# Attention with cluster masks and two expert layers: the first key tile's transposed probabilities split on Pool, and the reciprocals' broadcast in one operation

## The chip, the cores and the metric

The kernel runs on one core of one Trainium2 chip. The core has five engines that run side by side, each through its own list of instructions in order: TensorE (PE in the rows, with its weight loads as PEld), VectorE (DVE), ScalarE (ACT), GpSimd (Pool, POOL in the rows) and SyncE (SP, which only issues DMAs here). An engine that waits for another holds up everything behind the waiting instruction in its own list. The metric is the device time of one execution in microseconds, lower is better.

## What is computed

```python
# attention: q, k, v of (2, 8, 768, 64), centroids of (8, 16, 64)
q_assign = argmax(einsum('bhsd,hcd->bhsc', normed(q), normed(centroids)))   # k_assign likewise
mask = q_assign[:, :, :, None] == k_assign[:, :, None, :]
scores = where(mask, q @ k.T / sqrt(64), -1e9)
attn = exp(scores - max(scores)); attn = attn / (sum(attn) + 1e-9)
x = (attn @ v)                       # put together to 1536 tokens x 512
# expert layer 1, w_in 512 x 2048, w_out 2048 x 512
h = x @ w_in;  x = (h * cos(h)) @ w_out
# expert layer 2, same sizes
h = x @ w_in2; g = where(h >= 1, h, where(h <= -1, 0, (h + 1)**2 / 4)); out = g @ w_out2
```

## The kernel before

Matrix products are made in a 32-bit format that PE rounds its inputs to (FP32R). To keep precision each operand is split into a high part (the number rounded to that format) and a low part (the number less its high part), and the products of the parts are summed in PSUM. So almost every operand needs two operations ahead of its matmul: a rounding copy and a subtraction.

The attention stage goes over 8 pairs of heads (2 batches, 4 pairs each, numbered from 0). A pair is prepared (`prep_pair`): the queries and keys are transposed and split, their dot products with the centroids are made (`dots`), the largest is found and made into one-hot rows (`eq`, L382 on DVE, L383 on Pool; `dots`, L390 on DVE), these are transposed on PE (`po`, L410) and copied by ACT (`oht`, L430) into the score operands, and the values are split on Pool (`vv`, L403 and L404).

Then come 4 units of a pair: one head and one half of the 768 query rows (384) each, 32 units in all, numbered through. A unit has six slots, one for each tile of 128 keys (`kt` 0 to 5). What a unit needs: scores in PSUM (`s`, L453 and L456 on PE), the row maxima (`nm`, L462 on DVE), the exponentials with their row sums (`p`, `den`, L471 on ACT), and in each slot three transposes of the probabilities into one PSUM tile of 128 x 384 (`pt`, L499 on PE), its high part (`phi`, L502, a copy by ACT) and its low part (`plo`, L507, a subtraction on DVE that reads the PSUM tile again), and two matmuls of `vv` with these parts that sum into `o` (L517, L518). The PSUM pool of these tiles has three buffers, which `pt`, `po` and some others share. The loop over slots runs ahead: scores are made 8 slots before the slot whose transposes need them, and the weighted sums (`p_v`) stand 4 slots or less behind their transposes, as PV_AT says:

```python
        PV_AT = (4, 4, 5, 6, 7, 8)
```

At the end of a unit `inverse` adds the small constant to the three row sums on Pool (`den`, L481), takes their reciprocals on DVE (L482), and spreads each over 64 columns on Pool (`rb`, L486, three operations). When both heads of a pair are through one half, `finish` transposes `rb` on PE (`r`, L541), adds the two parts of the result on Pool (`xt`, L543), multiplies by the transposed reciprocals on DVE (`xt`, L544), and splits the product on Pool (`xh`, L547; `xl`, L551).

The order in which an engine meets these is not that of the code alone: a scheduler puts each engine's list in order from the loop's order and its own idea of durations, so a changed instruction can move others. Preparing a pair begins 12 slots before the pair's first unit, so that its last steps (`eq`, `vv`, `po`) fall together with the finishing of the pair before: this stretch, six times in the run, is called a change of pairs here, and named by the pair that is being prepared.

Behind attention come the two expert layers (L603 on), dense matmuls with the hidden products split on Pool and DVE; the 64-bit weights are converted by DVE, ACT and Pool on the way (L134 to L161), two chunks of them already during attention.

Of the kernel before, what the change touches and what calls it, by code (L numbers as in the profile page):

```python
# [8 lines left out]
F32 = mybir.dt.float32  # L9
# [4 lines left out]
AF = mybir.ActivationFunctionType  # L14
ALU = mybir.AluOpType
# [3 lines left out]
P = 128  # L19
# [13 lines left out]
def attention_moe_moe(  # L33
# [18 lines left out]
    nc = tc.nc  # L52
    B, H, S, D = q.shape
# [3 lines left out]
    NJ = S // P  # L57
    HJ = NJ // 2
    HS = S // 2
# [9 lines left out]
    cpool = ctx.enter_context(tc.tile_pool(name="cpool", bufs=1))  # L69
# [2 lines left out]
    desc = cpool.tile([P, C], F32, name="desc")  # L72
    for c in range(C):
        nc.gpsimd.memset(desc[:, c:c + 1], float(C - c))
    ones = cpool.tile([P, D], F32, name="ones")
    nc.gpsimd.memset(ones, 1.0)
    ohscale = cpool.tile([P, 1], F32, name="ohscale")
    ohbias = cpool.tile([P, 1], F32, name="ohbias")
    for r in range(4):
# [25 lines left out]
    def later(n, f, *args):  # L105
        due.setdefault(now[0] + n, []).append((f, args))
# [85 lines left out]
    with ExitStack() as actx:  # L192
        ap = actx.enter_context(tc.tile_pool(name="apool", bufs=1))
# [271 lines left out]
        def row_exp(n):  # L465
            s, nm = ptile[n]
            u, jj = divmod(n, HJ)
            if jj == 0:
                dens[u] = ap.tile([P, HJ, 2], F32, tag="den", bufs=4, name=f"den{u}")
            p = ap.tile([P, 2, HS], F32, tag="p", bufs=P_BUFS, name=f"p{n}")  # L470
            nc.scalar.activation(p, s[:, :, :HS], AF.Exp, bias=nm,  # L471
                                 accum_out=dens[u][:, jj, 0:1])
            ptile[n] = p
            if jj == HJ - 1:
                later(2, inverse, u)

        def inverse(u):

            i, h, hf = units[u]
            den = dens.pop(u)  # L480
            nc.gpsimd.tensor_scalar(den[:, :, 0], den[:, :, 0], 1e-9, 1.0, ALU.add, ALU.mult)  # L481
            nc.vector.reciprocal(den[:, :, 1], den[:, :, 0])  # L482
            if h == 0:
                rb[(i, hf)] = ap.tile([P, HJ, 2, D], F32, tag="rb", bufs=2, name=f"rb{i}_{hf}")
            for jj in range(HJ):
                nc.gpsimd.tensor_scalar(rb[(i, hf)][:, jj, h], ones, den[:, jj, 1:2], 1.0,  # L486
                                        ALU.mult, ALU.mult)

        dens = {}
        rb = {}  # L490
# [4 lines left out]
        def p_transpose(u, kt):  # L495
            ps = ps_t.tile([P, HS], F32, tag="t", name=f"pt{u}_{kt}")
            for jj in range(HJ):
                p = ptile[u * HJ + jj].rearrange("p a n -> p (a n)")
                nc.tensor.transpose(ps[:, jj * P:(jj + 1) * P], p[:, kt * P:(kt + 1) * P], ident)  # L499
            hi = ap.tile([P, HS], F32R, tag="phi", bufs=6, name=f"phi{u}_{kt}")  # L500
            lo = ap.tile([P, HS], F32R, tag="plo", bufs=6, name=f"plo{u}_{kt}")
            nc.scalar.activation(hi, ps, AF.Copy)  # L502
            pts[(u, kt)] = (hi, lo, ps)

        def p_lo(u, kt):
            hi, lo, ps = pts[(u, kt)]
            nc.vector.tensor_tensor(lo, ps, hi.bitcast(F32), ALU.subtract)  # L507

        def p_v(u, kt):
            i, h, hf = units[u]  # L510
            vv = prepped[i][0]
            hi, lo, _ = pts.pop((u, kt))
            if kt == 0:
                opsum[u] = ps_o.tile([P, HS], F32, tag="o", name=f"o{u}")
            o = opsum[u]
            lhs = vv[:, kt, h * P:(h + 1) * P]
            nc.tensor.matmul(o, lhs, hi, start=(kt == 0), stop=False)  # L517
            nc.tensor.matmul(o, lhs, lo, start=False, stop=(kt == NJ - 1))  # L518
            if kt == NJ - 1:
                later(1, o_parts, u)  # L520

        def o_parts(u):
# [31 lines left out]


        LEAD, PREP, PREP1 = 8, 12, -3
        PV_AT = (4, 4, 5, 6, 7, 8)
        NSLOT = len(units) * NJ
        PAIR = 4 * NJ
        ct = centroid_load()  # L560
# [7 lines left out]

        pv_slots = {}
        for u in range(len(units)):  # L570
            for kt in range(NJ):
                pv_slots.setdefault(u * NJ + PV_AT[kt], []).append((u, kt))
        preps = []
        prep_at = {(i - 1) * PAIR - PREP: i for i in range(2, len(pairs))}
        prep_at[PREP1] = 1
        for slot in range(-max(LEAD, PREP), NSLOT + PV_AT[-1] - NJ + 1):
            g = slot + LEAD
            if slot in prep_at:
                preps.append(prep_pair(prep_at[slot]))
            if 0 <= slot < NSLOT:  # L580
                p_transpose(slot // NJ, slot % NJ)
            if 0 <= g < NSLOT:
                scores(g // 2, g % 2)
            for u, kt in pv_slots.get(slot, ()):
                p_v(u, kt)
            if slot % 2 == 0:
                for s in (slot - 1, slot):
                    if 0 <= s < NSLOT:
                        p_lo(s // NJ, s % NJ)
                if 2 <= g < NSLOT + 2:  # L590
                    row_exp(g // 2 - 1)
            next_slot()
            if slot == 60:
                issue_chunk(0)
            preps = [p for p in preps if next(p, 0) != 0]
            if NSLOT - 6 * CHUNK <= slot < NSLOT and slot % 3 == 0:
                pump(1)
            if slot % 2 == 1 and 0 <= g < NSLOT:
                row_max(g // 2)
# [142 lines left out]
```

## Time and profile before

| | |
|---|---|
| median of 3 runs | 826.47 us (824.32 to 827.69) |
| profiled execution | 821.31 us, of which the span from first to last instruction is 819.5 us |
| busy share of the span | PE 97%, PEld 81%, DVE 77%, ACT 51%, Pool 33% |
| instructions | PE 4042, PEld 4043, DVE 957, ACT 794, Pool 442 |
| attention stage | about 20 to 284 us; the expert layers fill the rest |

A busy share counts the time in which an instruction of the engine runs; PE's matmuls overlap, so its share is no measure of how fast they run. The shares are means over the whole span: DVE, ACT and Pool work mostly in the first third. In the rows, times are in microseconds from the span's start, `out<-in` are the program's tiles without their numbers, and what stands in brackets is the engine's idle time just before the instruction and what ended it.

### The profile page before, as it was taken

To read this page: it belongs to the slowest core of one execution; us is meant where nothing else is said; L and a number is where in the kernel's file an instruction comes from. 1 tells how busy PE (TensorE), PEld (TensorE's weight loads), DVE (VectorE), ACT (ScalarE), POOL (GpSimd) and SP (SyncE) were. 2 spreads that over 40 slices of the span, in tenths; PEclk is the share of its full clock that TensorE was granted. 3 is DMA by queue.
4 is the path that set the end of the run, shared out by engine and by line. 5 is a ranking of instruction groups with operands and counts; after the bars stand their busy time and mean duration, and the time that the engine had idled before them with its cause. 6 is when DMAs were issued, how large, how long until landed. Compare 5 with 4: busy or idle time off the path is not lost.

```text
span 819.5 us, 11332 instructions
## 1 busy us (share of the span) xinstructions
PE 798.6 (97%) x4042; PEld 665.8 (81%) x4043; DVE 633.6 (77%) x957; ACT 417.1 (51%) x794; POOL 270.4 (33%) x442
## 2 busy tenths in 40 slices
PE   7899999999999999999999999999999999999998
PEld 4788888988888887888888888888888888888886
DVE  5779899899898686787878778887876987755552
ACT  3788888897889764444343424223434233222220
POOL 3356655577553241222211211442231122111110
PEclk9999999999999999999999999999999999999999
DMA  7847556446540002222131222121122121000012
GB/s 145 192 89 155 142 121 166 101 107 137 137 89 33 1 15 89 102 70 85 51 104 52 103 58 97 52 88 67 52 59 96 56 89 62 1 1 0 14 50 92
DMA packets 48183, 65.97 MB, mean 80 GB/s; under 512 B 27904, under 2 KB 32640, under 8 KB 48128
## 3 DMA queue, kind: packets, MB, share of 16 engines
q1 hardware_dynamic: 46432, 64.83, 29.0%
q10 hardware_dynamic: 1696, 0.43, 0.3%
q8 instruction: 32, 0.52, 0.3%
q14 instruction: 23, 0.19, 0.1%
HBM read 43.02 MB, written 3.15 MB: 56 GB/s over the span
## 4 chain that ended last, share of the span: by engine, by line
PE 62%; DVE 1%; ACT 1%; POOL 1%; issue 0%; POOLq 0%
PE y L654 11%; PE y L653 11%; PE y L652 11%; PE h L653 10%; PE h L654 10%; PE h L652 10%; DVE gl L614 0%; DVE r L622 0%; POOL gh L610 0%; DVE g L627 0%; ACT L623 0%; ACT r L623 0%; DVE w L160 0%; ACT n L621 0%; ACT wx L144 0%
## 5 line engine op out<-in xcount | busy, mean ns | idle before, releaser
L610 POOL TENSOR_SCALAR gh<-g 128x512 fp32r<-128x512 f32 x96 | 70.8, 738 | 292.4 <-DVE g L641 165.3
L653 PE MATMUL h<-xl,w 128*128 128x512 f32 x384 | 151.5, 395 | 0.0
L652 PE MATMUL h<-xh,w 128*128 128x512 f32 x384 | 151.5, 395 | 0.0
L654 PE MATMUL h<-xh,w 128*128 128x512 f32 x384 | 151.4, 394 | 0.0
L507 DVE TENSOR_TENSOR plo<-pt,phi 128x384 fp32r<-128x384 f32 x192 | 99.8, 548 | 16.9 <-ACT phi L502 15.6
L502 ACT ACTIVATE phi<-pt 128x384 fp32r<-128x384 f32 x192 | 91.2, 493 | 21.0 <-PE pt L499 19.1
L637 ACT ACTIVATE p<-h,mone 128x512 f32<-128x512 f32 x48 | 33.0, 688 | 134.4 <-DVE m L636 134.0
L499 PE MATMUL pt<-ident,p 128*128 128x128 f32 x576 | 96.7, 278 | 4.3 <-DVE plo L507 2.8
L462 DVE TENSOR_REDUCE nm<-s 128x1 f32<-128x768 f32 x96 | 90.7, 946 | 6.9 <-PE s L456 6.3
L471 ACT ACTIVATE p<-s,nm 128x768 f32<-128x768 f32 x96 | 86.8, 904 | 12.8 <-DVE nm L462 12.5
L614 DVE TENSOR_TENSOR gl<-g,gh 128x512 fp32r<-128x512 f32 x96 | 71.1, 741 | 20.0 <-POOL gh L610 15.0
L654 PEld LDWEIGHTS h<-xh,w 128*128 128x128 f32 x384 | 71.9, 187 | 17.6
L653 PEld LDWEIGHTS h<-xl,w 128*128 128x128 f32 x384 | 71.9, 187 | 17.5
L652 PEld LDWEIGHTS h<-xh,w 128*128 128x128 f32 x384 | 71.9, 187 | 17.5
L144 ACT ACTIVATE wx<-wraw 128x1024 f32<-128x1024 f32 x32 | 36.4, 1138 | 95.6 <-DMA wraw<-in_moe_w_in_dram 35.8
L453 PE MATMUL s<-st,st 128*128 128x384 f32 x192 | 78.7, 411 | 4.2 <-ACT p L471 3.6
L499 PEld LDWEIGHTS pt<-ident,p 128*128 128x128 f32 x576 | 69.2, 140 | 15.1 <-DVE plo L507 3.1
L654 PE MATMUL y<-gh,w 128*128 128x512 f32 x192 | 74.9, 390 | 1.2 <-DVE w L160 1.2
L691 DVE TENSOR_TENSOR acc<-y,acc 128x512 f32<-128x512 f32 x72 | 49.3, 685 | 33.5 <-PE y L654 33.5
L653 PE MATMUL y<-gl,w 128*128 128x512 f32 x192 | 74.9, 390 | 0.0
L653 PE MATMUL y<-w,gh 128*128 128x512 f32 x192 | 74.9, 390 | 0.0
L652 PE MATMUL y<-gh,w 128*128 128x512 f32 x192 | 74.8, 390 | 0.0
(118 smaller groups left out, 1641.7 us busy)
## 6 DMA issues: line engine op xcount, KB each, us to landing
wraw<-in_moe_w_in_dram SPq DMA_DIRECT2D x16, 1024.0 KB, 5.2
wraw<-in_moe_w_out_dram SPq DMA_DIRECT2D x16, 1024.0 KB, 4.9
st<-t SPq DMA_DIRECT2D x24, 192.0 KB, 4.4
st<-th SPq DMA_DIRECT2D x9, 384.0 KB, 3.9
st<-tl SPq DMA_DIRECT2D x18, 192.0 KB, 4.1
st<-th SPq DMA_DIRECT2D x18, 192.0 KB, 4.2
nat<-in_q_dram SPq DMA_DIRECT2D x8, 384.0 KB, 5.3
natv<-in_v_dram SPq DMA_DIRECT2D x8, 384.0 KB, 4.7
```

Of the source, the lines that this page charges most:

```text
L453: nc.tensor.matmul(s[:, step, :HS], qt[:, 0, cols], kt[:, 0, kc], start=True, stop=False)
L462: nc.vector.tensor_reduce(nm, s[:, :, :HS], AX.XY, ALU.max, negate=True)
L471: nc.scalar.activation(p, s[:, :, :HS], AF.Exp, bias=nm, accum_out=dens[u][:, jj, 0:1])
L499: nc.tensor.transpose(ps[:, jj * P:(jj + 1) * P], p[:, kt * P:(kt + 1) * P], ident)
L502: nc.scalar.activation(hi, ps, AF.Copy)
L507: nc.vector.tensor_tensor(lo, ps, hi.bitcast(F32), ALU.subtract)
L610: nc.gpsimd.tensor_scalar(hi, g, 1.0, 0.0, ALU.mult, ALU.add)
L614: nc.vector.tensor_tensor(lo, g, hi.bitcast(F32), ALU.subtract)
L652: nc.tensor.matmul(o, lh, rh, start=first, stop=False)
L653: nc.tensor.matmul(o, lh, rl, start=False, stop=False)
L654: nc.tensor.matmul(o, ll, rh, start=False, stop=last)
L691: nc.vector.tensor_tensor(a, po, a, ALU.add)
```

## The change

The first key tile of each unit (POOL_KT = 0) is split on Pool: ACT copies its PSUM tile into a 32-bit tile `p32` in SBUF, Pool makes the high part from it, and then the low part. DVE's subtraction for that tile goes. The weighted sums of a unit begin with key tiles 1 and 2 and take tile 0 third. The three operations that spread the reciprocals become one that reads the reciprocals as a broadcast. The tile of ones goes.

```diff
-    ones = cpool.tile([P, D], F32, name="ones")
-    nc.gpsimd.memset(ones, 1.0)
...
-            for jj in range(HJ):
-                nc.gpsimd.tensor_scalar(rb[(i, hf)][:, jj, h], ones, den[:, jj, 1:2], 1.0,
-                                        ALU.mult, ALU.mult)
+            nc.gpsimd.tensor_scalar(
+                rb[(i, hf)][:, :, h], den[:, :, 1].unsqueeze(2).to_broadcast([P, HJ, D]),
+                1.0, 0.0, ALU.mult, ALU.add)
...
-            nc.scalar.activation(hi, ps, AF.Copy)
+            if kt == POOL_KT:
+                p32 = ap.tile([P, HS], F32, tag="p32", bufs=2, name=f"p32_{u}")
+                nc.scalar.activation(p32, ps, AF.Copy)
+                nc.gpsimd.tensor_scalar(hi, p32, 1.0, 0.0, ALU.mult, ALU.add)
+                nc.gpsimd.tensor_tensor(lo, p32, hi.bitcast(F32), ALU.subtract)
+                ps = None
+            else:
+                nc.scalar.activation(hi, ps, AF.Copy)
             pts[(u, kt)] = (hi, lo, ps)
 
         def p_lo(u, kt):
             hi, lo, ps = pts[(u, kt)]
+            if ps is None:
+                return
             nc.vector.tensor_tensor(lo, ps, hi.bitcast(F32), ALU.subtract)
...
-            if kt == 0:
+            first, final = kt == PV_ORDER[0], kt == PV_ORDER[-1]
+            if first:
...
-            nc.tensor.matmul(o, lhs, hi, start=(kt == 0), stop=False)
-            nc.tensor.matmul(o, lhs, lo, start=False, stop=(kt == NJ - 1))
-            if kt == NJ - 1:
+            nc.tensor.matmul(o, lhs, hi, start=first, stop=False)
+            nc.tensor.matmul(o, lhs, lo, start=False, stop=final)
+            if final:
...
-        PV_AT = (4, 4, 5, 6, 7, 8)
+        PV_ORDER, PV_AT = (1, 2, 0, 3, 4, 5), (4, 4, 5, 6, 7, 8)
+        POOL_KT = 0
...
-            for kt in range(NJ):
-                pv_slots.setdefault(u * NJ + PV_AT[kt], []).append((u, kt))
+            for kt, slot in zip(PV_ORDER, PV_AT):
+                pv_slots.setdefault(u * NJ + slot, []).append((u, kt))
```

The order on Pool at the change to pair 5 (unit 15 is ending, unit 16 is the first of pair 4; the number behind a tile's name is its unit, pair or pair and half). Before:

```order
L547 TENSOR_SCALAR xh_102<-xt1_3_0_2108 128x384
L486 TENSOR_SCALAR rb4_0_2436<-ones_80,den16_2312 128x64 x3
L551 TENSOR_TENSOR xl_103<-xt1_3_0_2108,xh_102 128x384
L383 TENSOR_TENSOR eq5_2422<-eq5_2422,desc_63 128x384
L403 TENSOR_SCALAR vv5_2550<-natv5_2042 128x6x64 x2
L404 TENSOR_TENSOR vv5_2550<-natv5_2042,vv5_2550 128x6x64
L543 TENSOR_TENSOR xt0_3_1_2226<-xt0_3_1_2226,xt1_3_1_2227 128x384
L404 TENSOR_TENSOR vv5_2550<-natv5_2042,vv5_2550 128x6x64
L481 TENSOR_SCALAR den17_2457<-den17_2457 128x3
```

Of the changed kernel, the same place (its lines are L555 for `xh`, L483 for `rb`, L559 for `xl`, L381 for `eq`, L401 and L402 for `vv`, L551 for the sum `xt`):

```order
L555 TENSOR_SCALAR xh_100<-xt1_3_0_2106 128x384
L483 TENSOR_SCALAR rb4_0_2434<-den16_2310 128x3x64
L559 TENSOR_TENSOR xl_101<-xt1_3_0_2106,xh_100 128x384
L503 TENSOR_SCALAR phi16_0_2443<-p32_16_2445 128x384
L504 TENSOR_TENSOR plo16_0_2444<-p32_16_2445,phi16_0_2443 128x384
L381 TENSOR_TENSOR eq5_2420<-eq5_2420,desc_63 128x384
L401 TENSOR_SCALAR vv5_2546<-natv5_2038 128x6x64 x2
L402 TENSOR_TENSOR vv5_2546<-natv5_2038,vv5_2546 128x6x64 x2
L551 TENSOR_TENSOR xt0_3_1_2224<-xt0_3_1_2224,xt1_3_1_2225 128x384
L479 TENSOR_SCALAR den17_2455<-den17_2455 128x3
```

Two new operations stand ahead of `eq`, and the second L404 (now L402) stands ahead of the sum `xt` and no longer behind it.

The order on DVE at the same change, from the low parts of unit 16 on. Before:

```order
L507 TENSOR_TENSOR plo16_4_2511<-pt16_4_2506,phi16_4_2510 128x384
L544 TENSOR_TENSOR xt1_3_1_2227<-xt0_3_1_2226,r3_1_2525 128x384
L390 TENSOR_TENSOR dots5_2324<-eq5_2422,mx5_2421 128x384
L482 RECIPROCAL den17_2457<-den17_2457 128x3
L462 TENSOR_REDUCE nm54_2571<-s54_2513 128x1
L507 TENSOR_TENSOR plo16_5_2538<-pt16_5_2533,phi16_5_2537 128x384
L462 TENSOR_REDUCE nm55_2602<-s55_2580 128x1
L507 TENSOR_TENSOR plo17_0_2578<-pt17_0_2573,phi17_0_2577 128x384
```

Of the changed kernel, where L552 is the product that was L544, L388 was L390, L480 was L482, L460 was L462 and L514 was L507:

```order
L514 TENSOR_TENSOR plo16_4_2509<-pt16_4_2504,phi16_4_2508 128x384
L552 TENSOR_TENSOR xt1_3_1_2225<-xt0_3_1_2224,r3_1_2523 128x384
L388 TENSOR_TENSOR dots5_2322<-eq5_2420,mx5_2419 128x384
L480 RECIPROCAL den17_2455<-den17_2455 128x3
L460 TENSOR_REDUCE nm54_2567<-s54_2511 128x1
L460 TENSOR_REDUCE nm55_2600<-s55_2579 128x1
L514 TENSOR_TENSOR plo16_5_2536<-pt16_5_2531,phi16_5_2535 128x384
L514 TENSOR_TENSOR plo17_1_2594<-pt17_1_2589,phi17_1_2593 128x384
```

The low part of tile 0 is gone, and the second row maximum stands ahead of the low part of tile 5. The product and `dots` stay where they were, behind each other.

## Rows read from the trace of the kernel before

**Rows 1.** Busy time of each engine in the attention stage (first line: columns).

```profile
core 0: us, PE busy (x) PEld busy (x) DVE busy (x) ACT busy (x) POOL busy (x), PEclk, DMA share, GB/s
20.00:284.00 264.00, 252.13 (x1663) 225.61 (x1663) 231.04 (x397) 219.35 (x487) 145.81 (x262) 1.00 0.50 115
```

**Rows 2.** PE's waits: us, times, longest; from 20 to 284 us, then before 60.

```profile
PE s L453 <- ACT p L471: 3.6, 11, 1.3
PE pt L499 <- DVE plo L507: 2.8, 6, 1.1
...
PE s L453 <- ACT p L471: 1.8, 3, 1.3
```

**Rows 3.** Timeline of Pool at the change to pair 5: start, duration.

```profile
160.59 0.51 POOL L547 TENSOR_SCALAR xh<-xt 128x384 fp32r<-128x384 f32 x1 [1.23 <-DVE den L482]
161.09 0.90 POOL L486 TENSOR_SCALAR rb<-ones,den 128x64 f32<-128x64 f32 x3
161.95 1.00 POOL L551 TENSOR_TENSOR xl<-xt,xh 128x384 fp32r<-128x384 f32 x1
163.44 1.01 POOL L383 TENSOR_TENSOR eq<-eq,desc 128x384 f32<-128x384 f32 x1 [0.49 <-DVE eq L382]
164.42 0.99 POOL L403 TENSOR_SCALAR vv<-natv 128x384 fp32r<-128x384 f32 x2
165.39 1.01 POOL L404 TENSOR_TENSOR vv<-natv,vv 128x384 fp32r<-128x384 f32 x1
166.35 1.03 POOL L543 TENSOR_TENSOR xt<-xt,xt 128x384 f32<-128x384 f32 x1
167.32 1.02 POOL L404 TENSOR_TENSOR vv<-natv,vv 128x384 fp32r<-128x384 f32 x1
```

**Rows 4.** Timeline of DVE at the same change.

```profile
162.28 1.08 DVE L382 TENSOR_TENSOR eq<-dots,mx 128x384 f32<-128x384 f32 x1
...
166.41 1.00 DVE L507 TENSOR_TENSOR plo<-pt,phi 128x384 fp32r<-128x384 f32 x2
167.41 0.55 DVE L544 TENSOR_TENSOR xt<-xt,r 128x384 f32<-128x384 f32 x1
167.88 0.88 DVE L390 TENSOR_TENSOR dots<-eq,mx 128x384 f32<-128x384 f32 x1
```

**Rows 5.** Timeline of PE at the same change.

```profile
168.91 0.52 PE L410 MATMUL po<-ident,dots 128*128 128x128 f32 x3
...
171.45 0.44 PE L453 MATMUL s<-st,st 128*128 128x384 f32 x1 [0.21 <-ACT p L471]
```

**Rows 6.** Groups of instructions from 20 to 284 us: count, busy us, mean ns, idle before.

```profile
L507 DVE TENSOR_TENSOR plo<-pt,phi 128x384 fp32r<-128x384 f32 x192 | 99.8, 548 | 16.9 <-ACT phi L502 15.6
...
L462 DVE TENSOR_REDUCE nm<-s 128x1 f32<-128x768 f32 x96 | 90.7, 946 | 6.9 <-PE s L456 6.3
...
L486 POOL TENSOR_SCALAR rb<-ones,den 128x64 f32<-128x64 f32 x96 | 30.1, 332 | 5.6 <-DVE den L482 5.6
...
L382 DVE TENSOR_TENSOR eq<-dots,mx 128x384 f32<-128x384 f32 x7 | 6.1, 877 | 0.0
...
L390 DVE TENSOR_TENSOR dots<-eq,mx 128x384 f32<-128x384 f32 x7 | 4.9, 695 | 0.0
```

**Rows 7.** Timelines of Pool and DVE at the changes to pairs 3 and 7.

```profile
97.25 1.01 POOL L383 TENSOR_TENSOR eq<-eq,desc 128x384 f32<-128x384 f32 x1 [0.50 <-DVE eq L382]
...
102.16 0.56 DVE L544 TENSOR_TENSOR xt<-xt,r 128x384 f32<-128x384 f32 x1 [0.78 <-POOL xt L543]
...
230.03 0.99 POOL L403 TENSOR_SCALAR vv<-natv 128x384 fp32r<-128x384 f32 x2 [0.28 <-PE o L518]
...
232.92 1.01 POOL L543 TENSOR_TENSOR xt<-xt,xt 128x384 f32<-128x384 f32 x1
...
234.29 0.54 DVE L544 TENSOR_TENSOR xt<-xt,r 128x384 f32<-128x384 f32 x1
```

**Rows 8.** Timelines of Pool and PE behind the change to pair 5.

```profile
170.47 0.90 POOL L486 TENSOR_SCALAR rb<-ones,den 128x64 f32<-128x64 f32 x3
...
174.94 0.34 PE L517 MATMUL o<-phi,vv 128*128 128x384 f32 x1
```

## Prediction

> **What bounds the kernel now.** I read the busy time of the attention stage first. From 20 to 284 us TensorE (PE) is recorded busy for 252.1 of 264 us, VectorE (DVE) for 231.0, ScalarE (ACT) for 219.4 and GpSimd (Pool) for 145.8, at full clock [rows 1]. The reader is to see that four engines share this stage, that none of them has much room except Pool, and that Pool is the one that gets work. The change leaves the code of the two expert layers behind it alone, so I look for its effect here. Then I read PE's own waits: over the whole stage the recorded idle time that names ACT's exponentials is 3.6 us and that which names DVE's low parts is 2.8 us [rows 2]. A wait for an exponential is often a wait for DVE at one remove, since the exponential needs DVE's row maximum. So a lighter DVE can give back at most about 3.6 + 2.8 = 6.4 us, 0.8% of the time, whatever it saves.
>
> Last I read the timelines of one change of pairs, where everything meets: Pool multiplies `eq`, makes the value parts `vv` of the next pair and finishes the old one (`xt`, `xh`, `xl`) [rows 3]; DVE runs behind it [rows 4]; PE waits for DVE [rows 5]. The reader is to see three things. Pool's run from `xh` (160.59) to the end of the sum `xt` (166.35 + 1.03 = 167.38) has one hole, 0.49 us before `eq`. DVE takes up L544, which reads that sum, at 167.41, exactly when its own two low parts are done (166.41 + 1.00): neither engine has spare time there. And PE begins the transposes `po` at 168.91, just behind DVE's L390 (167.88 + 0.88 = 168.76). What is late on Pool here is late on PE.
>
> **The change, part by part.** *DVE loses 32 low parts.* One of six L507 goes in each of the 32 units: 548 ns each [rows 6], 500 ns apart where two stand together [rows 4], so 16 to 17.5 us of DVE's 231.0.
>
> *ACT* keeps its count: the copy of the first key tile has the same shape and only another output, so nothing. That PSUM bank comes free after the copy and no longer after DVE's subtraction; this helps the same waits as the lighter DVE, and is in their 6.4 us.
>
> *Pool gains two operations for each unit.* The trace has the same two kinds at this size: the one-input L403 on 128x384, two of them in 0.99 us, so 0.49 each, and the two-input L404, 0.96 us from its start to the next [rows 3]; together 1.45 us. *The broadcast* goes from three L486 of 128x64, 0.90 us together or 332 ns each [rows 6], to one of 192 elements. No row shows that size; it lies between one 128x64 (0.33) and one 128x384 (0.49). I take 0.41, and the saving is 0.90 - 0.41 = 0.49 us (0.41 to 0.57). So Pool has about 1 us more per unit, 31 us in all, on 145.8 of 264: it fits in sum.
>
> *Where it doesn't fit.* The order puts `phi16_0` and `plo16_0` on Pool ahead of `eq`, and at this change it also puts both L404 ahead of the sum `xt`, where one of them stood behind it. From `xh` on, in steps from start to start (the last with its whole duration): `xh` 0.50, broadcast 0.41, `xl` 1.00, the two new ones 1.45, `eq` 0.98, L403 0.97, two L404 1.92, `xt` 1.03: 8.26 us. Before it was 167.38 - 160.59 = 6.79. The hole of 0.49 us swallows what the broadcast doesn't. So DVE gets the sum 1.47 us later, and since L544 stands on DVE ahead of L390, the reciprocal and the row maxima `nm54` and `nm55`, all of these wait; PE stands at `po` meanwhile, with its transposes, scores and weighted sums queued behind. The cover that DVE had, its own low parts up to 167.41, gets shorter by the low part taken away.
>
> The change of pairs before this one has the same rows and the same new order: 1.47 us again. For pair 7 the hole before L403 was 0.28 us and L544 came 234.29 - (232.92 + 1.01) = 0.36 us after Pool's sum [rows 7]; one L404 moves ahead too: 1.45 + 0.96 - 0.49 - 0.28 - 0.36 = 1.3. For pair 3 both L404 were ahead already, the hole was 0.50 us, and DVE waited 0.78 us for Pool's sum even so [rows 7]: 1.45 - 0.49 - 0.50 = 0.5. For the two that are left (pairs 2 and 6) the order keeps one L404 behind; between nothing and 0.5 each, I take 0.2 for both. Sum: 1.47 + 1.47 + 1.3 + 0.5 + 0.2 = 4.9 us. PE's own lag is a little less where L390 runs shorter than the 0.88 us it took here (695 ns in the mean [rows 6]): I take nine tenths, **+4.4 us** (3.8 to 4.9).
>
> *What the lighter DVE gives back.* The bound is 6.4 us. 1.8 us of that lies before 60 us [rows 2], in the ramp, where the first exponentials gate PE, and I count PE's stops at the changes of pairs (`po` and the score matmul at 171.45 [rows 5]) as staying, since they hang on Pool's sum. From what is left I take **-2.5 us**, and keep 0 and 6.4 as ends.
>
> *Sum:* +4.4 - 2.5 = +1.9 us. The profiled execution took 821.31 us (819.5 span); the runs' median is 826.47, 5.2 above. I move both alike: 823.2 and **828.4 us**.
>
> **A rule set against the rows.** Of two-input DVE operations on 128x384, L507 reads one input from PSUM and takes 548 ns; L382, both of whose inputs lie in SBUF, takes 877 ns in the mean [rows 6], and 1.08 us where it begins beside Pool's `xl` (162.28, `xl` runs to 162.95) [rows 3, 4]. The Trainium skill, "SBUF — State Buffer", section "SBUF: two separate sides", says that a DVE operation with two SBUF inputs and a GpSimd operation that reads SBUF exclude each other for whole instructions. By that rule, the trace agrees, the low parts taken off DVE never blocked Pool, while the new ones on Pool can block L382 and L390; it speaks against the change. By the rows alone: if all seven L382 and seven L390 of the stage rose to 1.08 us from 0.877 and 0.695, DVE would take 7 x 0.20 + 7 x 0.39 = 4.1 us more, all of it at changes of pairs. My sum has none of it, since L390 then mostly waits behind a Pool that has just ended its run.
>
> **Rivals.** *Faster.* DVE, 88% busy, is the real pacemaker, and PE's buffers bridge Pool's delay. For it: DVE has no hole in rows 4. Against: Pool's sum and L544 meet at the same moment, and PE follows L390 by 0.15 us. It would give the full 6.4 less a third of the 4.4: about 826.5 - 5 = 821.5.
>
> *Slower.* Pool's run at the changes of pairs becomes the pacemaker and nothing comes back, because after each change PE runs dense and only stops where Pool or ACT is late. It decides as soon as DVE idles over 1 us before L552 at four or more changes. Price: +4.9, and one L462 of 0.95 us [rows 6] where the low part `plo16_5`, which now stands behind both row maxima, holds PE up: 826.5 + 6 = 832.5.
>
> *Slower by exclusion.* L382 and L390 wait out Pool's longer run as reckoned above: 1.9 + 4.1 = +6, also 832.5. For it L382's 1.08 us; against it that most of these already collide.
>
> *Pool's parts come too late for their own matmul.* At the worst place, unit 17, Pool ends the broadcast at 170.47 + 0.90 = 171.37, and PE's third weighted sum, where the order now puts key tile 0, begins at 174.94 [rows 8]. Less 1.45 + 1.47 - 0.49 that leaves 1.1 us. It holds; each microsecond beyond it would cost some 1 us at six changes, 834.
>
> **How the numbers follow.** No change that can be told (within 0.5%, which is 4.1 us and about what a measurement of this kernel can tell): 0.50. Faster rival 0.20. Slower by Pool's run 0.20, by exclusion 0.08, by late parts 0.02, together 0.30. The likeliest gives 828.4. Low end: all of the 6.4 back against part of the 4.4, and some scatter of the runs: 822. High end: +4.9 with the exclusion's larger half or the second slower case: 834.
>
> **What would show it.** Right: DVE idle before L552 and waiting for Pool's L551 at the changes of pairs, 4 to 6 us in all (0.8 before, at pair 3); Pool's new operations at 0.5 and 1.0 us, the broadcast near 0.41; DVE busy down by some 17 us in the stage; PE's waits elsewhere for low parts nearly gone. Wrong: L552 without a wait, or PE's `po` late without any effect on the end of attention; L382 and L390 above 1 us throughout; PE waiting for Pool at the new matmuls; or a shift that begins only in the expert layers, which the sum leaves out.

## Result: 833.0 us, slower by 1.07%

Over seven runs each, the changed kernel took 833.04 us in the median (830.33 to 836.54) and the kernel before 824.32 us; the ratio is 1.0107, with a 95% interval of 1.0081 to 1.0132. The forecast time was 828.4 us, the likeliest case "no change that can be told". The range up to 834 held the result, the likeliest case did not. That the range held is in part luck: it was written around 826.47 us, the kernel before's median of three runs, which over seven runs is 824.32. As a ratio 834 stands for +0.91%, less than the 1.07% measured.

The profiled execution took 832.11 us, with a span of 830.3 us: 10.8 us more than that of before, which at 821.31 us was faster than any of the seven timed runs of that kernel. One yardstick serves for all that follows, the **attention stretch**: from the start of the first of the 96 row maxima `nm` to the start of the last. It leaves out what differs ahead of the first from run to run. These are the rows of that line in the traces of before and of after (durations in ns, then first and last start in us):

```profile
L462 DVE TENSOR_REDUCE nm<-s x96: 925/947/959, 21.0 to 275.0; 128x1 f32<-128x768 f32 x96
```

```profile
L460 DVE TENSOR_REDUCE nm<-s x96: 927/948/960, 21.0 to 285.6; 128x1 f32<-128x768 f32 x96
```

It lasted 254.0 us and lasts 264.6 now: 10.6 of the 10.8 us are lost between the first and the last row maximum, and next to nothing in the expert layers. First the groups of instructions of after that answer to [rows 6], from 20 to 300 us (count, busy us, mean ns, idle time before them and what ended it):

```profile
L514 DVE TENSOR_TENSOR plo<-pt,phi 128x384 fp32r<-128x384 f32 x160 | 84.5, 550 | 18.9 <-ACT phi L507 18.4
L552 DVE TENSOR_TENSOR xt<-xt,r 128x384 f32<-128x384 f32 x16 | 8.8, 550 | 8.5 <-POOL xt L551 7.7 <-PE r L549 0.7
L388 DVE TENSOR_TENSOR dots<-eq,mx 128x384 f32<-128x384 f32 x7 | 5.4, 775 | 0.0
L380 DVE TENSOR_TENSOR eq<-dots,mx 128x384 f32<-128x384 f32 x7 | 4.2, 606 | 0.0
L386 DVE TENSOR_REDUCE mx<-eq 128x24 f32<-128x384 f32 x7 | 3.9, 552 | 7.1 <-POOL eq L381 7.1
...
L483 POOL TENSOR_SCALAR rb<-den 128x192 f32<-128x192 f32 x32 | 12.6, 393 | 2.8 <-DVE den L480 2.8
```

DVE has 99.8 - 84.5 = 15.3 us less of low parts, a little under the forecast of 16 to 17.5. It spends 7.7 us idle for Pool's sum `xt` and 7.1 us for its product `eq`. One wait of 2.6 us for the sum, behind the last row maximum, stands in the trace of before as well; the other 12.2 us compare with 0.8 + 0.3 = 1.1 us of before:

```profile
L544 DVE TENSOR_TENSOR xt<-xt,r 128x384 f32<-128x384 f32 x16 | 8.8, 547 | 3.4 <-POOL xt L543 3.4
...
L388 DVE TENSOR_REDUCE mx<-eq 128x24 f32<-128x384 f32 x7 | 3.8, 542 | 0.4 <-POOL eq L383 0.3
```

The timelines of the change to pair 5, Pool and then DVE, answer to [rows 3, 4]:

```profile
167.54 1.39 POOL L559 TENSOR_TENSOR xl<-xt,xh 128x384 fp32r<-128x384 f32 x1
168.90 0.51 POOL L503 TENSOR_SCALAR phi<-p 128x384 fp32r<-128x384 f32 x1
169.49 1.01 POOL L504 TENSOR_TENSOR plo<-p,phi 128x384 fp32r<-128x384 f32 x1
170.47 1.00 POOL L381 TENSOR_TENSOR eq<-eq,desc 128x384 f32<-128x384 f32 x1
171.44 0.99 POOL L401 TENSOR_SCALAR vv<-natv 128x384 fp32r<-128x384 f32 x2
172.40 1.97 POOL L402 TENSOR_TENSOR vv<-natv,vv 128x384 fp32r<-128x384 f32 x2
174.33 1.01 POOL L551 TENSOR_TENSOR xt<-xt,xt 128x384 f32<-128x384 f32 x1
...
167.51 0.55 DVE L380 TENSOR_TENSOR eq<-dots,mx 128x384 f32<-128x384 f32 x1
...
171.50 0.55 DVE L386 TENSOR_REDUCE mx<-eq 128x24 f32<-128x384 f32 x1 [1.18 <-POOL eq L381]
...
175.37 0.56 DVE L552 TENSOR_TENSOR xt<-xt,r 128x384 f32<-128x384 f32 x1 [1.52 <-POOL xt L551]
```

Pool runs without a hole from `xl` to the sum, and DVE stands twice: before the second maximum, and before the product with the sum. TensorE follows DVE, in the timeline of the same change:

```profile
173.53 0.52 PE L497 MATMUL pt<-ident,p 128*128 128x128 f32 x3 [0.50 <-DVE plo L514]
...
176.53 0.52 PE L408 MATMUL po<-ident,dots 128*128 128x128 f32 x3 [1.03 <-DVE den L480]
```

Over the whole stage (20 to 290 us) TensorE's waits in after, which answer to [rows 2], are (us, times, longest):

```profile
PE s L451 <- ACT p L469: 4.3, 11, 1.3
PE pt L497 <- DVE plo L514: 3.5, 4, 2.0
PE po L408 <- DVE den L480: 3.1, 3, 1.0
```

The waits for exponentials and for low parts, 3.6 and 2.8 us before, haven't shrunk with DVE's load, and the wait at `po`, which follows DVE's queue at the changes, has come up from 0.3 us.

The second thing to see is TensorE's clock, which [rows 1] had at 1.00 throughout. Three stretches of after (us, busy time of each engine, granted clock, DMA share, GB/s):

```profile
38.71:42.12 3.41, 3.41 (x14) 3.22 (x13) 2.05 (x4) 1.64 (x3) 1.19 (x2) 0.50 1.19 252
103.56:106.97 3.41, 3.41 (x14) 3.31 (x13) 3.34 (x7) 1.48 (x3) 2.94 (x5) 0.50 0.98 211
199.13:202.55 3.42, 3.42 (x16) 3.32 (x16) 2.81 (x5) 1.83 (x4) 2.28 (x2) 0.50 1.04 336
```

Here the clock is at the lower of its two levels, 1.2 GHz, and TensorE is busy throughout, so each stretch can cost up to half of itself, 1.7 us. Shortly ahead of each, TensorE had waited:

```profile
38.35 0.60 PE L497 MATMUL pt<-ident,p 128*128 128x128 f32 x3 [2.40 <-ACT p L502]
...
103.25 0.60 PE L497 MATMUL pt<-ident,p 128*128 128x128 f32 x3 [2.03 <-DVE plo L514]
...
197.67 0.27 PE L350 MATMUL pd<-cn,th 128*128 128x64 f32 x1 [1.21 <-DVE plo L514]
```

The first of these waits was 1.12 us long before, where DVE's low part freed the bank that the transposes need:

```profile
36.92 0.52 PE L499 MATMUL pt<-ident,p 128*128 128x128 f32 x3 [1.12 <-DVE plo L507]
```

Now ACT's copy frees it, and that copy stands on ACT behind an exponential which itself waits for a row maximum. ACT's rows:

```profile
36.92 0.90 ACT L469 ACTIVATE p<-s,nm 128x768 f32<-128x768 f32 x1 [3.42 <-DVE nm L460]
37.72 0.19 ACT L469 ACTIVATION_READ_ACCUMULATOR p<-s,nm 128x1 f32 x1
37.81 0.48 ACT L502 ACTIVATE p<-pt 128x384 f32<-128x384 f32 x1
```

### The profile page after: what moved, and what is told of

The parts are those of the page before. It is cut to its first block, busy times and chain, and to the rows that moved or that the text cites. A ratio compares the mean times of both kernels' runs of the same rounds, so it can differ in the third digit from the quotient of the medians.

```text
span 830.3 us, 11225 instructions
## 1 busy us (share of the span) xinstructions
PE 801.2 (96%) x4043; PEld 669.2 (81%) x4043; DVE 620.8 (75%) x925; ACT 418.3 (50%) x794; POOL 304.8 (37%) x441
## 4 chain that ended last, share of the span: by engine, by line
PE 61%; DVE 1%; ACT 1%; POOL 1%; issue 0%; POOLq 0%
PE y L663 10%; PE y L662 10%; PE y L661 10%; PE h L663 10%; PE h L662 10%; PE h L661 10%; DVE gl L623 0%; DVE r L631 0%; POOL gh L619 0%; DVE g L636 0%; ACT n L630 0%; ACT L632 0%; ACT r L632 0%; DVE w L158 0%; ACT wx L142 0%
## 5 line engine op out<-in xcount | busy, mean ns | idle before, releaser
L497 PE MATMUL pt<-ident,p 128*128 128x128 f32 x576 | 98.9, 280 | 7.1 <-DVE plo L514 3.5
L460 DVE TENSOR_REDUCE nm<-s 128x1 f32<-128x768 f32 x96 | 90.5, 948 | 15.4 <-PE s L454 14.5
L514 DVE TENSOR_TENSOR plo<-pt,phi 128x384 fp32r<-128x384 f32 x160 | 84.5, 550 | 18.9 <-ACT phi L507 18.4
L507 ACT ACTIVATE phi<-pt 128x384 fp32r<-128x384 f32 x160 | 76.1, 493 | 20.7 <-PE pt L497 19.4
L662 PEld LDWEIGHTS h<-xl,w 128*128 128x128 f32 x384 | 71.9, 187 | 17.5
L661 PEld LDWEIGHTS h<-xh,w 128*128 128x128 f32 x384 | 71.9, 187 | 17.5
L662 PE MATMUL y<-w,gh 128*128 128x512 f32 x192 | 74.8, 390 | 0.0
L661 PE MATMUL y<-w,gh 128*128 128x512 f32 x192 | 74.7, 389 | 0.0
```

Of the source, the lines that this page charges most:

```text
L460: nc.vector.tensor_reduce(nm, s[:, :, :HS], AX.XY, ALU.max, negate=True)
L661: nc.tensor.matmul(o, lh, rh, start=first, stop=False)
L662: nc.tensor.matmul(o, lh, rl, start=False, stop=False)
```

## Experiments

Twelve kernels, each timed beside the kernel before. "Stretch" is the attention stretch of the one profiled execution (254.0 before, 264.6 after), "drops" the clock drops within it. One execution need not be typical: the profiled one of e5 is the fastest of its six runs, those of e4 and e8 are the slowest of theirs.

| kernel | median us | ratio to before, 95% | stretch us | drops |
|---|---|---|---|---|
| e1 no split | 825.77 | 1.0018 [0.9997, 1.0039] | 254.6 | 0 |
| e2 not at changes | 826.02 | 1.0023 [1.0002, 1.0043] | 256.0 | 1 |
| e3 only at changes | 830.86 | 1.0072 [1.0045, 1.0099] | 261.6 | 1 |
| e4 PE filled | 833.65 | 1.0121 [1.0092, 1.0150] | 265.5 | 0 |
| e5 values late | 829.23 | 1.0076 [1.0052, 1.0099] | 257.8 | 1 |
| e6 before, values late | 823.05 | 0.9999 [0.9982, 1.0015] | 254.1 | 0 |
| e7 split behind `eq` | 832.02 | 1.0101 [1.0082, 1.0121] | 262.6 | 1 |
| e8 both moves | 823.85 | 1.0015 [0.9993, 1.0037] | 257.5 | 2 |
| e9 split where free | 821.19 | 0.9972 [0.9954, 0.9990] | 253.0 | 0 |
| e10 broadcast alone | 824.69 | 1.0007 [0.9990, 1.0025] | 254.7 | 0 |
| e11 start filled | 819.78 | 0.9946 [0.9932, 0.9961] | 252.1 | 0 |
| e12 e9 and e11 | 818.36 | 0.9940 [0.9918, 0.9961] | 250.9 | 0 |

Where a kernel's stretch grows against before is seen by the n-th row maximum: its start in the one trace less its start in the other, both from the first. A star marks a part with a clock drop (us):

```
part (row maxima)          after    e1     e2     e3     e5     e7     e8     e9
start-up       (1-10)      1.9*   -0.5    1.8*   0.0    2.1*   0.9    2.6*   0.3
change to 2    (10-28)     1.0     0.7    1.2    1.6    0.7    1.0    0.2    0.2
change to 3    (28-40)     1.8*   -0.6   -1.2    1.8*   0.3    0.3   -0.8   -1.2
change to 4    (40-52)     1.4     0.1    0.0    1.6    0.2    1.5   -0.1   -0.1
change to 5    (52-58)     1.5     0.0    0.0    1.5    0.2    1.5   -0.1   -0.1
change to 6    (58-76)     2.3*    1.0    1.0    1.0    0.8    2.7*   2.5*   0.3
change to 7    (76-96)     0.7    -0.1   -0.8    0.0   -0.5    0.7   -0.8   -0.5
```

The column of e1, which has the new order and the broadcast but no split, shows what a part can shift by without the split: up to 0.7 us, and 1.0 us at the change to pair 6.

**Which units cost.** Three kernels split the change up.

```diff
-            if kt == POOL_KT:
+            if kt == POOL_KT and u < 0:                               # e1
+            if kt == POOL_KT and not (u % 4 == 0 and 4 <= u <= 24):   # e2
+            if kt == POOL_KT and u % 4 == 0 and 4 <= u <= 24:         # e3
```

> The changed kernel without its Pool split: kt = 0 is split by ACT and DVE as before, the order of products (1, 2, 0, 3, 4, 5) and the one-operation broadcast stay. Theory A (the lost time is Pool's phi and plo standing ahead of Pool's other work at the changes of pairs, plus TensorE clock drops that follow the longer waits): all of it goes, the time is that of before or up to 3 us below it (the broadcast saves 0.5 us of Pool a unit), 821 to 825 us, granted clock 1.0. Rival B (the new order of the products is what costs, since kt = 0 now enters third): the time stays near 832 us.

> The changed kernel with the split left to ACT and DVE in units 4, 8, 12, 16, 20 and 24, whose Pool run stands ahead of the mask product, the values' parts and the sum xt at each change of pairs; the other 26 units keep Pool's split. Theory A: most of the waits at changes go (about 5 us of the loss) and so do the clock drops near 103 and 199 us; what is left is the wait near 36 us with its drop, and some of DVE's relief in the other units is kept: 822 to 827 us. Rival C (the copy on ACT and the Pool run cost something in every unit): about 26/32 of the loss stays, 831 us.

> The changed kernel with Pool's split in units 4, 8, 12, 16, 20 and 24 alone. Theory A: the loss at the changes stays and the relief of DVE between them is gone, so 830 to 835 us, with clock drops after the longest waits. Rival C (a cost of every unit): 6/32 of the loss, 825 to 826 us.

Theory A held, though e1's time is 0.8 us above its range. Without the split, or with it in the 26 units away from the changes, the kernel is within a quarter of a per cent of before; with it in the six units at the changes alone it is slower by 0.72%. At the changes to pairs 4 and 5 e3 loses 1.6 and 1.5 us, after 1.4 and 1.5, e2 nothing. So 26 more units with a lighter DVE give nothing back there. At the changes to pairs 3 and 7 they do give something: e2's stretch has 0.5 and 0.7 us less there than e1's. The order of the products (e1) costs nothing that can be told. One run of e3 and two of e1 had a mean granted clock of 1.00, so no drop to speak of: 827.27 against 821.83 and 821.87 us. The split at the six changes thus costs some 5.4 us by itself, without drops.

**The clock drops.** The places of the three waits get products to do.

```diff
+        FILL0, FILL1 = {7: 6}, {51: 5, 116: 3}
+            for _ in range(FILL0.get(slot, 0)):
+                scores((g - 1) // 2, (g - 1) % 2, False)
...
+            for _ in range(FILL1.get(slot, 0)):
+                scores(g // 2, g % 2, False)
```

> The changed kernel with 14 score products issued once more (the same operands into the same place, 0.36 us a pair) at the three places where TensorE waited 2.4, 2.0 and 1.2 us and its clock then went to 0.5: six repeats near 36 us, five near 101 us, three near 196 us. They run inside the waits, so by themselves they should cost under 1 us. Theory A with the clock (each drop of 3.4 us costs some 1.7 us and comes from the wait ahead of it): the drops at these places go, and 3 to 5 us with them, 828 to 830 us. Rival D (the drops come from something else, such as Pool's or ACT's load, or do not matter since TensorE waits for others then): clock and time as in the changed kernel or later, 832 to 834 us.

Half a miss. The stretch has no drop any more, but no time came back, and 833.65 us is what rival D had for it: the 14 repeats take 14 x 0.36 = 5.0 us, and waits came back behind them, as this row of PE shows, 5 us after the first six:

```profile
47.35 0.52 PE L497 MATMUL pt<-ident,p 128*128 128x128 f32 x3 [2.09 <-DVE plo L514]
```

No drop followed that wait of 2.1 us. So each drop seen inside attention began within a wait of over 1 us or up to 1.9 us behind one, but not each such wait brings one: one of 2.0 us near 103 us in e5 and one of 2.5 us near 41 us in e7 brought none. What a drop costs was not isolated by an experiment. An estimate from two executions of e3: the profiled one, with a drop at the change to pair 3 and one ahead of attention that made its first row maximum 2.6 us late, took 831.29 us, the run at a granted clock of 1.00 took 827.27, which leaves 4.0 - 2.6 = 1.4 us for the drop in attention. One run of the changed kernel shows a mean granted clock of 0.944 and was no slower than the others (832.03 us); what happened in it stays open.

**Sum or mask product.** e5 and e6 move the values behind the sum and the next denominator, in the changed kernel and in the one before; e7 moves Pool's split behind `eq`; e8 does both.

```diff
+        def values_after(i, values):
+            with tc.issue_after(xsum[i - 2]), tc.issue_after(dsum[4 * i - 3]):
+                values()        # the four operations on vv, then load_v(i + 1)
...
+                if u % 4 == 0 and 4 <= u <= 24:     # e7, e8
+                    later(SPLIT_LATE, pool_split, p32, hi, lo, u // 4 + 1)
```

> The changed kernel with the split of the values (two copies and two differences, some 3 us of Pool) moved behind Pool's sum xt and the next denominator at each change of pairs, so that xt and the denominator stand right behind Pool's phi, plo and the mask product. Theory X (what costs at a change is the sum xt, late behind phi, plo and the values): the loss of 8.7 us goes nearly whole and more, since the sum stood behind the values before the change too: 821 to 825 us. Theory E (it is the mask product eq, behind phi and plo, that DVE's second maximum waits for): nothing changes there, 831 to 834 us.

> The kernel before with the same move of the values' split behind the sum xt and the next denominator; nothing of the change. Theory X: TensorE's three waits at each change (0.55, 0.50 and 0.45 us in the trace of before) shrink, 3 to 5 us less in all: 819.5 to 822 us. Theory E, or another wait that takes their place: as before, 824 us.

> The changed kernel with Pool's phi and plo of units 4, 8, 12, 16, 20 and 24 moved behind the mask product eq; the sum xt still stands behind phi, plo and the values. Theory E: TensorE's wait of 0.65 us and DVE's of 1.2 to 2.1 us before the second maximum go, 4 us or more in all with the clock drops they led to: 826 to 829 us. Theory X: DVE waits the same time in front of the product of xt, 831 to 834 us.

> Both moves in the changed kernel: eq first, then phi and plo, then the sum xt and the denominator, then the values. If X and E each hold for a part, this is the fastest of the three, 820 to 823 us. If the lighter DVE (16 us less work) is worth anything once the waits at the changes are gone, it is below the kernel before with late values; if it is worth nothing, the two are the same within 0.3%.

At the changes to pairs 4 and 5, where no drop blurs the reading, e5 takes 1.4 and 1.5 us down to 0.2 and 0.3; e7 leaves them at 1.5. The waits of DVE say why. In e7 the second maximum no longer waits (first line), but the product with the sum waits all the longer (second); in e8 (third and fourth) neither waits, but for the 2.6 us at the end that stood in before too:

```profile
L388 DVE TENSOR_REDUCE mx<-eq 128x24 f32<-128x384 f32 x7 | 3.8, 542 | 0.5 <-POOL eq L382 0.5
L561 DVE TENSOR_TENSOR xt<-xt,r 128x384 f32<-128x384 f32 x16 | 8.8, 548 | 12.2 <-POOL xt L560 7.8 <-PE h L673 2.6 <-PE pt L504 1.3
```

```profile
L575 DVE TENSOR_TENSOR xt<-xt,r 128x384 f32<-128x384 f32 x16 | 8.7, 544 | 3.3 <-POOL xt L572 2.6 <-PE r L570 0.7
...
L393 DVE TENSOR_REDUCE mx<-eq 128x24 f32<-128x384 f32 x7 | 3.8, 539 | 0.2 <-POOL eq L387 0.2
```

So the sum decides at these two changes (theory X), and `eq` is worth the last 0.3 us once the sum is early. At the change to pair 3 it is not so: there e5 and e7 both come down from 1.8 us, which holds a drop, to 0.3 without one, although e5 keeps a wait of 2.1 us for `eq` and e7 one of 1.9 us for the sum. Theory X's figure for the time of e5 was missed by 4 us: the start-up part stayed at 2.1 us, and the runs slower than the profiled one had lower clocks (0.994 to 0.988, against 0.998). e8's 823.85 us missed its range of 820 to 823, and it is the same as e6 within 0.3%, so its time shows no worth of the lighter DVE. For e6 theory X was wrong. In that kernel Pool has the sum ready early, and DVE takes it up only when its own work is done:

```profile
168.79 1.01 POOL L555 TENSOR_TENSOR xt<-xt,xt 128x384 f32<-128x384 f32 x1 [0.19 <-ACT xt L543]
...
171.49 0.54 DVE L558 TENSOR_TENSOR xt<-xt,r 128x384 f32<-128x384 f32 x1
```

1.7 us lie between the end of the sum, 169.80, and its use. In the kernel before both engines are late at once: making Pool later costs (after), making it earlier alone gains nothing (e6).

**The two places left, and the broadcast.** e9 is e8 with units 0 to 3 and 17 to 19 unsplit too; 25 units keep Pool's split, the six at the changes (moved behind `eq`) among them, which the expectation's count of 19 leaves out. e10 is the broadcast edit alone.

```diff
+        SPLIT_LATE, NOSPLIT = 3, (0, 1, 2, 3, 17, 18, 19)
-            if kt == POOL_KT:
+            if kt == POOL_KT and u not in NOSPLIT:
```

> The kernel with both moves, and with Pool's split left to ACT and DVE also in units 0 to 3 (the wait of 2.4 us near 36 us, where the copy on ACT stands behind an exponential) and in units 17 to 19 (the wait of 1.2 us near 196 us). Theory A: these two places hold what was left of the loss (attention stretch 3.4 us longer than before, of it two clock drops), so the attention stretch comes to that of before within 0.5 us, no clock drop inside it, and the time to 821 to 823.5 us, whichever side of the kernel before. That it is clearly below the kernel before (by over 2 us) would say that DVE's lighter load in the other 19 units is worth something after all. Rival C (each split unit costs something): 19/32 of what is left stays, some 2 us.

> The kernel before with the one-operation broadcast alone. The three operations took 0.90 us and the one takes 0.35 us in the traces, 0.55 us of Pool in each of 32 units. Theory A: where the broadcast stands Pool is waited for at no place that counts, except at the changes, and there the sum's wait was worth nothing in the kernel before (late values gained nothing): 823 to 825 us, no change. Rival: the broadcast shortens Pool's run at the changes and gains up to 0.5 us at each of six, 820 to 821 us.

e9 met theory A in its time and is below both kernels: 0.28% faster than before, its stretch 1.0 us shorter, no drop in it. Only part of the 0.28% is the kernel's own: where the mean granted clock was 1.00, e9's four runs took 819.84 to 820.46 us and the three of the kernel before 821.32 to 821.57, some 1.3 us or 0.15%; the rest comes with how many runs had clock drops, at the start above all, and that e9 makes these rarer isn't shown. Here, with Pool's late work out of the way, DVE's lighter load in 25 units seems worth something: the stretch of e9 is 1.1 us shorter than that of e6, which has the move of the values but no split, and order and broadcast gave nothing by themselves (e1, e10). A kernel with order, broadcast and late values but no split was not run, so this is by difference and not shown. The broadcast alone changes nothing that can be told.

**The start.** e11 takes the kernel before and gives it seven more idle products, matmuls that nobody reads and of which the kernel has some at its start already; pair 1's values move too.

```diff
-NIDLE, IDLE1, IDLE2 = 13, 15, 6
+NIDLE, IDLE1, IDLE2, IDLE3 = 16, 15, 6, 4
+                    if i == 0 and s == 0 and hf == 1:
+                        run_idle(IDLE3, mm.ins if hasattr(mm, "ins") else mm)
...
+            later(VLATE, values_after, i, values)      # i == 1 only
```

> The kernel before with seven more idle products on TensorE at the start (three behind the first 13, four behind the first transposes, where it waited 0.73 and 0.84 us), and the split of pair 1's values behind the second denominator on Pool. In the runs in which the clock fell at the start it stayed at 0.5 for some 7 to 10 us and the first row maximum came 2.6 to 4.1 us later. If such a drop follows from those two waits, it becomes rare and the median nears that of undisturbed runs; the wait of 1.3 us near 35 us goes too: 819.5 to 822 us, faster by 0.3 to 0.5%. If the drop has another cause, or DVE's next step takes the wait's place: 823 to 825 us.

> The kernel of e9 (Pool's split in 19 units, values and split moved) with the edits of e11 (idle products at the start, pair 1's values behind the second denominator). If the gains are apart from each other they add: e9's attention stretch was 0.98 us shorter than that of before, e11's 1.93 us, and e11's start kept its full clock in most runs, so 817.5 to 819.5 us, 0.65 to 0.8% below the kernel before. If the one was already in the other (units 0 to 3 are unsplit, so the start's wait of 1.3 us is that of before), no double counting is seen either; a sum short of that by over 1 us says that the order of DVE and Pool between them changed again.

Both times held; e12's 0.60% is a little under the 0.65 to 0.8% expected. The drop at the start is seen in e1 (first line) and not in e11 (second), over the same time:

```profile
9.90:20.14 10.24, 9.99 (x39) 7.19 (x39) 6.19 (x15) 0.98 (x2) 4.53 (x5) 0.50 1.03 199
```

```profile
9.90:20.14 10.24, 8.62 (x53) 5.53 (x53) 7.27 (x18) 2.20 (x4) 4.66 (x5) 1.00 1.03 200
```

The mean granted clock of e11's twelve runs was 0.995 to 1.00, in eight of them 0.999 or more; that of the 29 runs of the kernel before beside them was 0.992 to 1.00, in three of them 0.999 or more, and with it their times ran from 827.39 down to 821.32 us. Which of the seven products did it is not shown: the first three didn't fill their wait in e11's trace, where it was 1.45 us (0.73 in that of before), the other four filled theirs of 0.84. The stretch is 1.9 us shorter, all of it by the tenth row maximum, where values of pair 1 no longer hold up the denominator. e12 adds the two: a stretch of 250.9 us and 818.36 us, the best version.

## Why the prediction was right or wrong

**What bounds the kernel: right in the main.** The whole shift arises in attention, most of it at the places named. That "neither engine has spare time there" is what e6 and the changed kernel show together.

**Pool's operations: right.** The two new ones last 0.51 and 1.01 us, from the first start to the next operation 170.47 - 168.90 = 1.57 us (1.45 forecast). The broadcast's median is 0.353 us, its mean 0.393 (0.41).

**Pool's delay, +4.4 us: the mechanism right, the sum a little small.** For pairs 4 and 5 I had 1.47 us each and the stretch grew by 1.4 and 1.5 us. For the others e3, which has the split at the changes alone, is to be held against e1, which has no split: 0.9 us at pair 2 (I had 0.2), 2.4 at pair 3 with a drop of up to 1.7 in it (0.5), next to nothing at pairs 6 and 7 (0.2 and 1.3). In all, without drops, the runs of e3 and e1 at full clock show 5.4 us. So the places were read rightly at pairs 4, 5 and 6, and that the sum comes near owes something to errors at the others that cancel. I followed the sum alone; `eq` is late by as much, and DVE's 7.1 us before the second maximum stood nowhere in the text. e7 shows that this wait by itself wasn't what counted at pairs 4 and 5, and e5 shows the same for pair 3, where it stayed at 2.1 us and 0.3 us was lost.

**What the lighter DVE gives back, -2.5 us: this step failed.** In sum it gave nothing. The changed kernel, with 32 split units, took 833.04 us and e3, with six of them, 830.86; its stretch is 3.0 us longer, with two more drops in it, and at the undisturbed changes to pairs 4 and 5 it loses the same. Of the 15.3 us that DVE saved, 11.1 became waiting for Pool. My bound of 6.4 us took TensorE's waits for exponentials and low parts to shrink with DVE's load, and I called the latter nearly gone; they are 4.3 and 3.5 us now, longer than the 3.6 and 2.8 before. Where something came out, at pairs 3 and 7 in e2 and at about 1 us in e9, Pool's late work was away from the changes or moved.

**What stood nowhere.** Two more places: the copy that frees the bank behind ACT's exponential near 36 us (I had put an earlier release down as a help), and the wait near 196 us, where DVE runs two steps on the weights, 1.53 and 1.56 us, ahead of a row maximum. And three clock drops of 3.4 us, up to 5 us in the profiled execution, by the estimate from e3 some 4.

**The rivals.** The slower one by Pool's run, at 0.20 and 832.5 us, comes nearest to what happened, though its price had neither `eq` nor the drops in it: DVE idles 1.5 us before L552 at three changes (4, 5 and 7), one fewer than I had set as the mark, and 2.1 and 1.5 us before L386 at the other two that cost most (3 and 6). The faster one is refuted by e3, in which Pool's delay is not bridged, and by e2. *By exclusion*: DVE didn't pay. L380 and L388 take 606 and 775 ns in the mean, together less than before [rows 6]. Where they meet, Pool paid: `xl`, begun 0.03 us behind L380, took 1.39 us. The Trainium skill, "SBUF — State Buffer", section "SBUF: two separate sides", says that whichever starts first keeps the ports for its whole instruction; the trace agrees, and I had charged it to the wrong engine. *Late parts*: no wait of PE for Pool's parts shows among its waits.

## What to carry to other kernels

An engine with room in its sum has none where its queue is what others wait for: before moving work to it, list what stands behind the new instructions at its fullest place, and everything that reads each of those. A saving on the engine that is relieved counts only where no other wait ends at the same moment; two engines that are late together are to be relieved together (Pool alone in e6, nothing; both in e9, a stretch 1 us shorter, by difference). If work is to move, put it where the receiving engine isn't waited for: 25 units and two moves turned a loss of 1.07% into a gain of 0.28%, of which some 0.15% stands at equal clock.

## What the hardware did that I had not expected

TensorE's clock fell to 1.2 GHz for 3.4 us in or shortly behind single waits of 1.2 to 3.1 us, in a stretch in which it was otherwise busy, but not behind each of them; by the estimate from e3 such a drop costs 1.4 us more, up to 1.7. At the start a drop of up to 10.2 us came in some runs and not in others: the kernel before's mean granted clock went from 0.992 to 1.00. With seven more idle products ahead of and within that stretch it became rare, and the median went from 824.5 to 819.8 us, of which the stretch accounts for 1.9. And one broadcast of 192 elements on Pool costs 0.35 us, about as much as one of 64 did (332 ns [rows 6]).
